# A linear-attention and MLP-mixer kernel on one core: Strassen products for the tail chunk, tail tokens twice in x, other engines for some evacuations, and an order written out job by job

## The chip, the cores and the metric

The kernel runs on one core of a Trainium2 chip. The metric is the device time of one execution in microseconds (us). Engines are named as in the profile: PE (TensorE), DVE (VectorE), ACT (ScalarE), POOL (GpSimd), SP (SyncE). Each has an instruction queue of its own that is worked off in order. A "bank" is one of PSUM's eight tiles of 128 x 512 fp32.

## The reference, cut to what matters

```python
def phi(x):                                   # q, k: batch 8, heads 8, tokens 576, head_dim 64; omega (128, 64)
    proj = einsum('bhsd,md->bhsm', x, omega)
    h = proj - sum(x*x, -1) / 2
    return exp(h - max(h, -1)) / sqrt(128)
q_p, k_p = phi(q * D**-0.25), phi(k * D**-0.25)
kv, z = einsum('bhsm,bhsd->bhmd', k_p, v), k_p.sum(2)
x = (einsum('bhsm,bhmd->bhsd', q_p, kv) / (einsum('bhsm,bhm->bhs', q_p, z) + 1e-6))   # -> (8, 576, 512)
h = relu(x.T @ w_tok1) @ w_tok2               # token mix, over the 576 tokens, 256 wide
u = x + h.T
out = u + relu(u @ w_ch1) @ w_ch2             # channel mix, 512 -> 1536 -> 512
```

## The kernel before, in words

The work is cut into eight batches. Of each batch's 576 tokens, 512 are its main part and 64 its tail. Main parts go through the channel mix as chunks 0 to 7; the tails of all eight batches together are a ninth chunk of 512 tokens, the tail chunk (chunk 8).

*Attention* (`attention`), per batch and pair of heads: kp (L729) and qp (L743) multiply by omega on 64 rows, one head on rows 0 to 63 and one on 64 to 127, side by side; L637 and L702 do so for the tails. ACT takes the exponentials (L605). DVE takes a maximum (km, L755) and its reciprocal, POOL scales v with it (vs, L762; for the tail vbd, L687), and PE makes kv from kp and vs (L775, L782), then the numerator and the denominator (num, L811 and L813). DVE divides and writes x (L820, L821). The fifth block of x holds the tail's 64 tokens; they stand on partitions 0 to 63 in even batches and on 64 to 127 in odd ones, beside rows made from a constant.

*Token mix* (`token_mix`): t1 is four matmuls with w1m and one with w1t per half of its output (L850, L851; in w1t the 64 rows of the other parity are zero), ACT's relu (L856), t2 (L868), then DVE's u = x + bank (L871). SP transposes u by DMA into uT (L876). Batch 0 has a form of its own (`token_mix_first`) that makes uT on PE. Every two batches, `token_tail` (L927) makes u of two tails.

*Channel mix* (`channel_mix`): c1 is 12 blocks of four matmuls of 512 columns on uT (L1031), each evacuated with a relu into r3 (L1051). For chunks 1 to 7, c2 is one level of Strassen's scheme (`channel_out_fast`): eight sums of halves of r3 on DVE (L961, tiles S and r3), then seven products of 12 matmuls of 256 columns (L994) in three banks, whose parts DVE reads and adds into the output tile o (L984). The sums of the weights (T1 to T4) are made once. Chunk 0 and the tail chunk use plain matmuls of 512 columns (L1072; the tail chunk's last quarter is split into 384 and 128), read by L1078 and L1081. SP stores o; the tail chunk's stores use SP and ACT.

*Loads.* Batches 0 and 1 come in through POOL's queue and are transposed on PE. For batches 2 to 7 POOL issues casts of q and k to fp16 in DRAM (L438, L443, L449), SP transposes them by DMA into qT and kT (L459), and POOL issues v (L416, and its tails, L430). Rings of three buffers hold qT, kT, v, x, u and uT.

*The order.* Each piece of work is a job with an engine, a cost, its dependencies, ring buffers that it takes and gives back, and a number from a list `TURN`. A planner (`Planner.run`) simulates the five engines with these costs and latencies and emits, of the jobs that could start first, the one with the lowest number; it fills PE's early waits with warm-up matmuls (L1124). Instructions then wait on semaphores where data or buffers demand it. POOL's loads are emitted in the order in which they are written. Three kinds of one-element POOL copies shape the loads in time: `touch_k` (L465) waits until kT of the batch has landed and stands ahead of that batch's load of v; `touch` (L471) waits until uT of batch b has landed, and the casts of batch b + 2 depend on it; `touch_u` (L477) waits for u of batch 1.

```python
load_transposed(b, b + key_of("lt", b), [touched.get(b - 2)])
load_v(b, b + key_of("lv", b), [touch_k(b, b + key_of("lv", b) - 0.05)] + ([touch_u(1, ...)] if b == NPE else []))
```

Of the kernel before, what the change touches and what calls it, by code (L numbers as in the profile page):

```python
# [21 lines left out]
TURN = [  # L22
    -15388, -7014, -13073, -46412, -7655, -14474, 12016, -15120, -18496, -8948, -22583, -7858, -7162, -43936, -2670,
    -3017, -3707, -7692, -13686, -20652, -22584, -5417, -6661, 23621, -1630, 152, -9786, 2937, -1379, -138, -4135,
    -255, 4012, -3019, 670, 2119, 30050, 19008, 6817, -16440, -9549, -63949, -1403, 26445, -14635, 15804, -8690,
    -63651, 24140, -58019, -2452, 24373, -36567, 21763, -1540, 3521, 18852, -60314, -19711, -30831, 6684, -19830,
    -11197, -21227, 25889, -24043, -11262, -14356, 3710, 6752, 14413, 23069, 5660, -15408, -27860, -2965, -7377,
    -9431, -12808, -52400, -38242, -37163, 3221, -15263, -20804, 22879, -13557, -55206, 13839, -49786, -6465, -202,
    4680, -47025, -14457, -46071, -53899, -9443, -9649, 8913, -19532, -37383, 814, -9792, -6427, -10267, -51100,
    15583, 27254, 1777, -46019, -50474, 376, 26739, 17561, -2105, -3193, 5465, -17463, 14213, -8969, 4853, -22951,  # L30
    19318, 1706, -24052, -49983, -13533, -6294, 24662, -12349, -49546, 5784, -3169, 5564, -50029, 26601, -30746,
    24843, -11451, -28569, -2751, 22527, 552, -6715, -14407, -15375, -15464, -19936, -52721, -17904, 3300, 12869,
    -15917, -13321, -9958, -1491, -4819, 646, -46682, -17992, -46784, -4826, 13594, -4048, 13343, 19470, 2741,
    -10090, 11772, 3497, -5567, -29390, 7254, 12676, 2776, -14376, 7802, 8337, 7031, -2161, -19859, -12732, -43413,
    -9916, -19216, -58973, 24369, -11565, 14103, -3033, -45480, -9352, 9592, 10185, -2540, 16827, 15484, -13557,
    -44120, -21483, -31242, -23901, 3400, -7003, -5296, -3805, -47459, -29837, -27877, -7451, -4247, 1753, -20557,
    2929, -1773, 21124, -1789, -25228, -1620, 18791, -664, -15420, -11225, -13389, -2744, 9408, 9845, 435, -135,
    22445, -3541, 13038, 5863, 20166, -10760, -19471, -21644, -601, -4056, -430, 14232, 4189, 10468, 10949, -3475,
    20422, -10178, 18794, -18465, -20798, 31084, -6838, 16566, 9681, -18602, 5577, 10752, -5297, -1849, 19149,
    -12929, -24198, -66020, -14908, -8184, -6166, -65205, 15276, -20150, 14963, -55181, -16990, -46958, -19935, 8099,  # L40
    -10665, 15556, 14406, 13591, 5438, -6274, 26511, 13520, 38954, 15603, -4947, 14565, 36526, 12763, 34929, 21853,
    37001, 15602, -6766, -6262, 14706, 15439, -13517, 15693, 21144, -1398, -6408, -6939, -8983, -13623, -8992, -9289,
    4719, -27010, -6574, -18136, 82, -2371, -17032, -9823, -27011, 8384, -6192, -16093, -17910, 7758, 14140, 108,
    -27948, -608, 8854, -3453, -10109, -11577, -13810, -12470, 3257, -14080, -8494, -10771, -11257, -16618, 3330,
    -17274, 3235, 1670, -16429, 7138, -2910, 2486, 3385, -13533, -59219, -9482, 8754, -17013, -8823, -6579, -11568,
    -9073, -5422, -2651, 5141, -1820, -13228, 11174, 2352, 10114, 10115, -14066, 1258, 4850, 33304, -25525, -22868,
    -25662, 1269, -8677, -14059, 7313, -16048, -12329, -4122, -16317, 2689, -25562, 22276, 4775, -18710, 10356, 496,
    -11758, 27399, -19583, 6689, -11186, -12765, -17338, -7597, -4698, -11639, -29139, -21982, 15114, -5787, -20076,
    -28319, -20689, -243, -14445, -11767, -19981, -10038, -5733, -16232, -14384, -3701, 6130, 4202, -3590, -23397,
    -3610, -22146, -2047, -7777, 3535, 11696, 3589, 14053, 2793, 349, 3537, 8491, 2220, -23014, 20063, -17210, 4249,  # L50
    11695, 709, 8460, 12020, 13969, -15424, 26804, -12046, 20202, -1874, 17391, 18744, -3467, -19446, 17390, -1859,
    16401, -22023, 9451, 4339, -22707, -17446, -26451, 2094, -15746, -4272, 14774, -19651, -7156, 112, -3587, -3434,
    -25433, 13873, 2630, 14048, -9769, 4425, -7075, -12087, -12522, -3917, 19581, -6390, -8901, -13427, -1181, 18678,
    -4045, 432, 13615, -5437, 13007, 1443, -10585, 9797, 2214, 7391, -2032, 12571, 1889, -3491, -6954, -29303,
    -23182, -29817, -24332, -2931, -7501, 14998, 8245, 10927, 2002, -11810, -21550, -14902, -7946, -26279, -1301,
    691, 11121, -3713, -6826, -4056, -2755, 26323, -554, 18902, -5970, -4993, -8453, -1366, 17640, 17804, 15115,
    19580, -5186, 6192, -134, 18765, 4162, 6381, 3651, 15911, 14780, -18160, -2045, 9672, -17660, 9621, -30386,
    -8188, -5144, -8187, -9411, 4616, 4852, 17834, 1462, -3139, 8840, -8896, 10423, -7338, 8960, 10376, -13163,
    17091, 13977, -8452, 16450, -30333, 9153, -8833, 13566, -28636, 10261, -5968, 9124, -2133, 30589, -41106, 8194,
    -1789, 1126, -6770, 5103, -6966, 8220, 1127, -17938, -9868, 11145, -13150, 10984, -2000, 29580, 27864, -15095,  # L60
    -4250, -10990, 13810, -46500, 13768, 21261, 18983, 2772, 2773, 3575, 16170, 30919, 2607, 14110, 16463, -2343,
    -18310, 8382, -7529, 16273, 30384, -516, 22171, -4626, -7305, 12970, 9221, 4737, -2165, -3253, 19048, 8805,
    10216, 19023, 13372, -12974, 11970, 19, 4449, -4866, 17204, -19334, -4013, 6176, -10560, -5347, 8886, -9214,
    -646, -5775, 6886, -8689, 1067, 6856, 3158, -2940, -8332, 5904, -7885, 13864, 6344, 8784, 6527, -8874, 3721,
    -206, -6079, -4129, 2648, -10216, 12686, 12078, -3004, -2224, 1638, -9213, -9825, -3812, 7751, -10988, -23199,
    -33491, 9689, -15345, -20536, -4352, -19859, 1333, -27862, -410, -18682, 15542, -7578, -16202, -5477, -6051,
    10330, 8738, 22953, -6008, 4920, -6176, -14218, 3475, 8079, -5905, -12788, 6217, 32716, -14997, 5159, 6270,
    25813, -10318, -10090, -5657, 7197, 7779, -13330, 7447, -8542, -9159, -3758, 22193, -6764, 27075, 6187, 8529,
    7206, 4308, 6524, -2156, 12129, -5827, -16280, -2630, 2881, 17984, 21000, 16285, 17051, 12562, -6502, -6544,
    -9527, 7971, 10323, 27175, -2021, 2054, 4848, -31261, -28426, -28130, -4079, 9328, -15259, 10054, -4167, -30516,  # L70
    -5759, -17236, 20912, -972, 4958, 21570, -3312, -18297, -2638, -50055, -1835, -47249, 413, -18400, -1670, -5520,
    -2170, -12900, 17150, 20837, -523, -31628, 6469, 112, -21361, 654, 18930, 13337, 6087, -6279, -2464, -8753,
    18192, 21341, 16066, -11343, -5800, -35522, 20880, 13337, -8965, 1896, -479, 1679, 5789, 288, -4811, 19118,
    25207, -1825, 11820, 16405, 20905, -43154, 11987, 27547, -4681, 10209, 8803, -2197, -8946, -3709, -17557, -8805,
    -10533, -16199, -27491, 16535, -8963, 26146, 1314, -18247, 9883, 6199, 1093, -19913, 4757, 16992, -476, 18685,
    -466, 9779, 4835, 4538, 16112, 22955, 25162, -26473, 1094, -15053, 8983, 23425, 18551, 15144, -2067, -14401,
    -25674, -3264, 19068, 21564, 19370, 21561, 19369, -369, 7251, 28795, 38558, 8305, -8220, 33607, 32424, -2369,
    -10808, -6295, -4563, -17410, -1230, 3456, 2605, 2422, 5647, 13207, 11405, 18208, 16281, -851, -32006, -9286,
    -3095, 9391, -1432, -1952, -5493, 20459, 11276, 9074, -1347, 12251, -21810, -7967, 8343, 6672, 9815, 569, -21526,
    15454, 8190, 9367, 7493, 16884, 728, 27655, -7207, -7903, 9589, 7508, 10012, 907, -13199, 6107, -5350, 16904,  # L80
    -4500, -12015, 7158, 26304, 6259, 24558, -3285, 10424, -716, -7436, -6436, -772, -35890, 3797, -17806, 10011,
    27243, 5135, 23103, -2409, -2140, -10265, 9455, 582, -7559, 6671, -13709, 2151, -15262, 8943, -20097, -5684,
    28560, -5089, -22380, 13833, -21820, -9450, 6234, 11702, 2636, -14448, -11523, 20648, 8829, -18231, -4520, 5423,
# [1073 lines left out]
```

## Time and profile before

| | |
|---|---|
| time, median of 3 runs | 282.66 us (282.34 to 283.93) |
| span of the profiled execution (first to last instruction) | 282.4 us; the page gives no other time of it |
| PE | busy 273.4 us (97%), granted clock 1.000 |
| DVE, ACT, POOL | busy 194.2, 158.6, 93.5 us |
| DMA | 39.63 MB, engines 0.8 to 1.0 busy for most of the first 200 us |
| first PE transposes start, last matmul starts | 4.67 us, 278.04 us |

The profile is one execution. "Busy" of PE counts modelled ends, and matmuls overlap by pipelining, so how long one holds the array is read from starts that follow each other. A chain line gives start, length, what, and a count. A group's or timeline's line gives line of the code, engine, operation, tile written <- tiles read, form, count, and in brackets the idle time before it with what ended it.

### The profile page before, as it was taken

Reading aid. Unit: us, or ns where it says so; the run is one execution under the profiler, and the core shown is the slowest. Engines: PE = TensorE matmul, PEld = TensorE weight load, DVE = VectorE, ACT = ScalarE, POOL = GpSimd, SP = SyncE. Lnnn points to the kernel's source line nnn. Section 1 sums busy time; section 2 is a strip of 40 time slices with the busy share of each in tenths; the row PEclk is TensorE's granted clock in tenths of the full one; section 3 lists DMA queues with packets and bytes.
Section 4 is the critical chain, followed back from the end, with each engine's and each line's share of the span. In section 5 each row is a group of like instructions: output and inputs, shape, how many; then the busy total and the mean of one; then the engine's idle time right before and its main releaser. Section 6 shows DMA issues by size and latency. Waiting matters only on the chain.

```text
span 282.4 us, 6126 instructions
## 1 busy us (share of the span) xinstructions
PE 273.4 (97%) x2437; PEld 166.1 (59%) x2437; DVE 194.2 (69%) x404; ACT 158.6 (56%) x329; POOL 93.5 (33%) x126
## 2 busy tenths in 40 slices
PE   7999999998999999999999999999999999999994
PEld 4577464443557656745567556655675477446761
DVE  3986959566798858694998576789796794034232
ACT  2987882098547663875576654875576511671200
POOL 8995950109312810256116501570151000000000
PEclk9999999999999999999999999999999999999999
DMA  8999999799963799989991997599963013300035
GB/s 190 199 202 191 202 217 160 176 190 148 229 91 77 155 190 151 124 217 148 157 151 61 205 209 110 105 194 228 149 91 152 0 22 74 149 2 0 0 151 149
DMA packets 83708, 39.63 MB, mean 140 GB/s; under 512 B 64160, under 2 KB 79904, under 8 KB 83488
## 3 DMA queue, kind: packets, MB, share of 16 engines
q0 software_dynamic: 34288, 17.45, 44.7%
q1 hardware_dynamic: 48608, 21.01, 33.3%
q10 hardware_dynamic: 784, 0.79, 0.9%
q8 instruction: 19, 0.31, 0.4%
q14 instruction: 9, 0.07, 0.1%
HBM read 35.88 MB, written 16.52 MB: 186 GB/s over the span
## 4 chain that ended last, share of the span: by engine, by line
PE 76%; DMA 9%; POOL 6%; DVE 6%; issue 2%; DVEq 0%; POOLq 0%
PE bank L1031 27%; PE bank L994 23%; PE bank L1072 5%; PE bank L850 4%; PE bank L868 4%; DMA uT<-u 3%; POOL vs L762 3%; DMA v<-in_v_dram 3%; DMA r<-in_k_dram 3%; PE bank L775 3%; PE bank L811 2%; DVE km L755 2%; PE bank L743 2%; PE bank L729 2%; PE bank L576 1%
## 5 line engine op out<-in xcount | busy, mean ns | idle before, releaser
L1051 ACT ACTIVATE r<-bank 128x512 f16<-128x512 f32 x106 | 63.0, 600 | 60.7 <-PE bank L1031 59.4
L1031 PE MATMUL bank<-uT,wc 128*128 128x512 f16 x376 | 88.6, 379 | 0.8 <-DMA uT<-u 0.8
L1031 PEld LDWEIGHTS <-wc 128*128 128x128 f16 x424 | 39.1, 98 | 41.0 <-DMA uT<-u 1.2
L605 ACT ACTIVATE qp<-bank 128x512 f16<-128x512 f32 x64 | 35.6, 624 | 19.1 <-PE bank L743 19.1
L755 DVE TENSOR_REDUCE km<-kp 128x8 f16<-128x1024 f16 x32 | 38.6, 1208 | 0.8 <-ACT kp L605 0.4
L605 ACT ACTIVATE kp<-bank 128x512 f16<-128x512 f32 x64 | 35.5, 627 | 6.3 <-PE bank L729 6.3
L762 POOL TENSOR_TENSOR vs<-v,vs 128x512 f16<-128x512 f16 x32 | 33.3, 1060 | 11.3 <-DVE vs L757 8.5
L994 PEld LDWEIGHTS <-r 128*128 128x128 f16 x336 | 32.2, 98 | 8.0 <-issue 1.3
L821 DVE TENSOR_TENSOR x<-bank,rc 128x320 f16<-128x320 f32 x62 | 30.5, 492 | 2.1
L984 DVE TENSOR_TENSOR o<-u,bank 128x512 f32<-128x512 f16 x28 | 19.0, 678 | 12.8 <-PE bank L994 12.8
L994 PEld LDWEIGHTS <-S 128*128 128x128 f16 x252 | 23.7, 98 | 6.3 <-issue 1.4
L820 DVE RECIPROCAL rc<-bank 128x5 f32<-128x5 f32 x62 | 11.6, 187 | 20.6 <-PE bank L813 19.6
L1072 PE MATMUL bank<-wc,r 128*128 128x512 f16 (+2 forms) x108 | 23.1, 356 | 0.0
L994 PE MATMUL bank<-wc,r 128*128 128x256 f16 x168 | 20.7, 273 | 0.0
L994 PE MATMUL bank<-T,r 128*128 128x256 f16 x168 | 20.7, 273 | 0.0
L994 PE MATMUL bank<-T,S 128*128 128x256 f16 x168 | 20.5, 273 | 0.0
L871 DVE TENSOR_TENSOR u<-x,bank 128x512 f16<-128x512 f16 x28 | 17.9, 682 | 1.2 <-PE bank L868 1.1
L687 POOL TENSOR_TENSOR vbd<-vt,vbd 128x512 f16<-128x512 f16 (+1 forms) x7 | 8.2, 1178 | 31.0 <-DVE vbd L678 8.0
L984 DVE TENSOR_TENSOR o<-o,bank 128x512 f32<-128x512 f32 x21 | 14.2, 676 | 6.0 <-PE bank L994 5.6
L465 POOL COPY junk<-kT 128x1 f16<-128x1 f16 x6 | 1.1, 189 | 49.3 <-DMA kT<-k 49.3
L961 DVE TENSOR_TENSOR S<-r 128x768 f16<-128x768 f16 x14 | 7.7, 552 | 13.7 <-ACT r L1051 13.6
L1072 PEld LDWEIGHTS <-r 128*128 128x128 f16 x108 | 9.9, 98 | 10.1 <-issue 0.7
(121 smaller groups left out, 391.1 us busy)
## 6 DMA issues: line engine op xcount, KB each, us to landing
out_dram<-o SPq DMA_DIRECT2D x14, 512.0 KB, 2.7
q<-in_q_dram POOLq DMA_DIRECT2D x6, 576.0 KB, 7.0
wc<-in_moe_w_ch_dram POOLq DMA_DIRECT2D x4, 768.0 KB, 12.0
k<-in_k_dram POOLq DMA_DIRECT2D x6, 512.0 KB, 8.1
v<-in_v_dram POOLq DMA_DIRECT2D x6, 512.0 KB, 6.5
r<-in_q_dram POOLq DMA_DIRECT2D x4, 256.0 KB, 7.2
v<-in_v_dram POOLq DMA_DIRECT2D x4, 256.0 KB, 7.2
out_dram<-o SPq DMA_DIRECT2D x4, 256.0 KB, 5.5
```

Source lines behind the costliest of these rows:

```text
L605: nc.scalar.activation(out=out, in_=in_, func=AF.Exp, bias=0.0, scale=1.0)
L755: nc.vector.reduce_max(out=mx, in_=kpv, axis=AX.X)
L762: nc.gpsimd.tensor_tensor(out=vs[:, :, 0:D], in0=t_v[place("v", b)][:, hh[0] : hh[0] + 2, :].rearrange("p h (j d) -> p (h j) d", d=D), in1 ...
L820: nc.vector.reciprocal(out=rc, in_=ps[:, :, :, D])
L821: nc.vector.tensor_tensor(out=t_x[place("x", b)][:, :, (2 * hp + hs[0]) * D : (2 * hp + hs[0] + n) * D].rearrange("p j (i d) -> p i j d", ...
L850: nc.tensor.matmul(ps, w1m[:, j, tb * P : (tb + 1) * P], x[:, j, :], start=(j == 0), stop=False)
L871: nc.vector.tensor_tensor(out=t_u[place("u", b)][:, j, :], in0=t_x[place("x", b)][:, j, :], in1=bank(n), op=ALU.add)
L984: nc.vector.tensor_tensor(out=o, in0=a, in1=ps, op=ALU.add)
L994: nc.tensor.matmul(ps[:, j * DH : (j + 1) * DH], a[:, cb, j * P : (j + 1) * P], w[:, cb, :], start=(b not in held and j == 0 and cb == 0), ...
L1031: nc.tensor.matmul(ps, wc1[:, db, cb * P : (cb + 1) * P], moving(db), start=(db == 0), stop=(db == ND - 1))
L1051: nc.scalar.activation(out=o, in_=bank(n), func=AF.Relu)
L1072: nc.tensor.matmul(ps[:, cols], r3[:, cb, j * P : (j + 1) * P], wc2[:, cb, cols], start=(cb == 0), stop=(cb == NCB - 1))
```

## The change

1. **Tail chunk by Strassen.** Chunk 8 goes through `channel_out_fast` too; the last of its seven products is split into two halves of six matmuls, with a read and a store each. u of the tails becomes one tile.
2. **Tail tokens twice in x.** qpt holds each tail token twice, so the fifth block of x has the tail on both halves of the partitions. w1t holds its 64 rows twice. For batches 1 to 7, t1's two matmuls with w1t become a pair on 64 rows each, ahead of the eight with w1m (jobs `t1_tail`). Batch 0 keeps a zero-padded copy (w1z).
3. **No copies that wait on DMA.** `touch_k`, `touch` and `touch_u` are gone. vbd of batches 0 and 1 moves into the tile T, and the constant rows of qpt are gone.
4. **Evacuations spread.** A table `MOVED` changes the engine of some 100 jobs: relus and copies between ACT and DVE, some vs from POOL to DVE, some Strassen sums from DVE to POOL, most stores of chunks 0 to 7 from SP to ACT's queue.
5. **New explicit order.** A list `ORDER` gives the jobs one by one over all engines (negative numbers are warm-up matmuls), and `SLOT` the ring buffers; no planner decides any more. POOL's loads may stand in any order.

The diff, cut to its core:

```diff
-    load_transposed(b, b + key_of("lt", b), [touched.get(b - 2)])
+    load_transposed(b, b + key_of("lt", b))
...
-    load_v(b, ..., [touch_k(b, ...)] + ([touch_u(1, ...)] if b == NPE else []))
+    load_v(b, b + key_of("lv", b))
...
+        for n in ORDER:
+            if n < 0:
+                self.warm(-1 - n)
+                continue
+            j = self.jobs[n]
...
+                    i = self.held[tag, name] = int(next(slots))
...
+    def engine(self, usual):
+        return MOVED.get(len(self.jobs), usual)
...
-    t_qpt = ring(COUNT["qpt"], [P, ST + SM + ST], FP16, "qpt")
+    t_qpt = ring(COUNT["qpt"], [P, H, 2, ST], FP16, "qpt")
...
-                exp(o[:, e], two(n_qt)[e][:, 0:256].rearrange("p (h r) -> p h r", h=H))
+                exp(o[:, e], two(n_qt)[e][:, 0:256].rearrange("p (h r) -> p h r", h=H).unsqueeze(2).broadcast_to((P, H, 2, RT)))
...
+        def t1_tail():
+            x = t_x[place("x", b)]
+            for tb in range(NT):
+                s = half[tb]
+                nc.tensor.matmul(bank(("h1", b, tb)), w1t[s, tb * P : (tb + 1) * P], x[s, NJ, :], start=True, stop=False)
...
-                    nc.tensor.matmul(ps, w1m[:, j, tb * P : (tb + 1) * P], x[:, j, :], start=(j == 0), stop=False)
-                nc.tensor.matmul(ps, w1t[:, b % 2, tb * P : (tb + 1) * P], x[:, NJ, :], start=False, stop=True)
+                    nc.tensor.matmul(ps, w1m[:, j, tb * P : (tb + 1) * P], x[:, j, :], start=False, stop=(j == NJ - 1))
...
-            on_act = c >= NPE or BY[("r0", "r1")[c]][cb] == "A"
+            e_relu = engine("ACT" if c >= NPE or BY[("r0", "r1")[c]][cb] == "A" else "DVE")
...
-                    (nc.gpsimd if on_pool else nc.vector).tensor_tensor(out=o[:, part], in0=a[:, part], in1=b[:, part], op=op)
+                    tt(e_sum, out=o[:, part], in0=a[:, part], in1=b[:, part], op=op)
...
-        fast = NPE - 1 <= c < B
+        fast = c >= NPE - 1
...
+            for j0, j1 in ((0, 1), (1, 2)) if tail and k == 6 else ((0, 2),):
```

More of the change, by code (lines that the diff above doesn't have):

```diff
@@ L228, in run @@
+        slots = iter(SLOT)
+        left, owner = {}, {}
+        for j in self.jobs:
+            for g in j.give:
+                left[g] = left.get(g, 0) + 1
+        for n in ORDER:
[3 more added lines that the diff above has]
+            j = self.jobs[n]
+            assert j.end is None and all(d.end for d in j.deps)
             for tag, name in j.take:
                 if (tag, name) not in self.held:
-                    i = self.find(tag)[0]
-                    self.places[tag][i] = math.inf
@@ L245, in run @@
+                    assert i < self.places[tag] and not left.get(owner.get((tag, i)))
+                    owner[tag, i] = (tag, name)
             j.fn()
+            j.end = True
             for g in j.give:
-                self.left[g] -= 1
-                self.freed[g] = max(self.freed.get(g, 0.0), j.end)
-                if self.left[g] == 0:
-                    self.places[g[0]][self.held[g]] = self.freed[g]
-        return max(at.values())
+                left[g] -= 1
+        assert all(j.end for j in self.jobs)
@@ L369, with copy, relu_to, tt @@
     src = {"q": q, "k": k}
+    def copy(eng, out, in_):
+        (nc.scalar.copy if eng == "ACT" else nc.vector.tensor_copy)(out=out, in_=in_)
+    def relu_to(eng, out, in_):
+        if eng == "ACT":
+            nc.scalar.activation(out=out, in_=in_, func=AF.Relu)
+        else:
+            nc.vector.tensor_relu(out=out, in_=in_)
+    def tt(eng, **kw):
+        (nc.gpsimd if eng == "POOL" else nc.vector).tensor_tensor(**kw)
     def bank(name):
@@ L661, in vbd @@
                 )
-            j_vbd0 = add("POOL", 2.15, HEAD["vbd"], vbd, deps=[j_mask, ld["vt", b]], take=[("vbd", b)], give=[("vt", b)])
+            e_vbd = engine("POOL")
+            j_vbd0 = add(e_vbd, 2.15, HEAD["vbd"], vbd, deps=[j_mask, *ld["vt", b]], take=[("vbd", b)] if dma_in else [], give=[("vt", b)])
         else:
@@ L989, in channel_out_fast @@
+        tail = c == B
+        outs = {}
         for k, (b, a_of, w, need) in enumerate(ops):
-            def go(k=k, b=b, a_of=a_of, w=w):
-                ps, a = bank((b, c)), a_of()
-                for j in range(2):
-                    for cb in range(NH):
-                        nc.tensor.matmul(ps[:, j * DH : (j + 1) * DH], a[:, cb, j * P : (j + 1) * P], w[:, cb, :],
-                                         start=(b not in held and j == 0 and cb == 0), stop=False, skip_group_check=True)
-                held[b] = True
@@ new lines, in channel_out_fast, with tail_rows, store @@
+        if tail:
+            def tail_rows(i, h, js, cols):
+                return out[4 * i : 4 * i + 4, SM:S, cols].rearrange("(j h) t d -> h t j d", h=2)[h][:, js, :]
+            ends = [(0, slice(0, 2), slice(0, DM), ["11", "12"], 0), (1, slice(0, 2), slice(DH, DM), ["22"], 0),
+                    (1, slice(0, 1), slice(0, DH), [("21", 0)], 0), (1, slice(1, 2), slice(0, DH), [("21", 1)], 1)]
+            for i, js, cols, need, two_queues in ends:
+                for h in range(2):
+                    eng = engine("ACT" if two_queues and h else "SP")
+                    def store(i=i, js=js, cols=cols, h=h, eng=eng):
+                        (nc.scalar if eng == "ACT" else nc.sync).dma_start(out=tail_rows(i, h, js, cols), in_=t_o[place("o", (c, i))][half[h], js, cols])
+                    dma(eng, key + 0.9, 0.3, store, deps=[outs[x] for x in need], give=[("o", (c, i))], cost=0.41)
+            return
@@ L1020, in channel_mix, with store @@
+        for i, need in ((0, ["11", "12"]), (1, [("21", 0), "22"])):
+            eng = engine("SP")
+            def store(i=i, eng=eng):
+                (nc.scalar if eng == "ACT" else nc.sync).dma_start(out=out[c, 0:SM, :].rearrange("(p j) d -> p j d", j=NJ)[:, 2 * i : 2 * i + 2, :], in_=t_o[place("o", (c, i))])
+            dma(eng, key + 0.9 + 0.1 * i, 1.3, store, deps=[outs[x] for x in need], give=[("o", (c, i))], cost=0.4)
     def channel_mix(c, key, jt):
@@ new lines, in channel_mix, with out_copy, store @@
+            k2 = key + 0.5 + 0.5 * (3 * j + 3) / 12
+            e_out = engine("DVE")
+            def out_copy(j=j, n=n, e_out=e_out):
+                copy(e_out, t_o[place("o", (c, j // 2))][:, j % 2], bank(n))
+            jo = add(e_out, 0.69, k2, out_copy, deps=[prev], take=[("o", (c, j // 2))], give=[("bank", n)])
+            eng = engine("SP")
+            def store(j=j, eng=eng):
+                (nc.scalar if eng == "ACT" else nc.sync).dma_start(out=out[c, j * P : (j + 1) * P, :], in_=t_o[place("o", (c, j // 2))][:, j % 2])
@@ L1094 @@
+            dma(eng, k2, 0.65, store, deps=[jo], give=[("o", (c, j // 2))], cost=0.4)
     for i in range(4):
```

430 lines of the change are left out of this document (148 added, 282 removed), and 134 rows, old and new, of tables (ORDER, TURN).

## The prediction

> **What bounds the kernel now.** I read the page first, parts 1 and 2.
>
> ```profile
> span 282.4 us, 6126 instructions
> PE 273.4 (97%) x2437; PEld 166.1 (59%) x2437; DVE 194.2 (69%) x404; ACT 158.6 (56%) x329; POOL 93.5 (33%) x126
> PEclk9999999999999999999999999999999999999999
> ```
>
> TensorE is busy 97% of the span at the full granted clock. So a gain has to come from fewer cycles in the matmul stream, or from its few gaps. Busy time hides how long a matmul holds the array, because ends are modelled (379 ns for 512 columns, L1031). The chain of waits, in order of time, shows it (start, length, what, count):
>
> ```profile
> 82.34 0.54 PE bank L743 x4
> ...
> 85.50 2.73 PE bank L994 x24
> ...
> 93.99 0.86 PE bank L1031 x4
> ...
> 271.21 7.17 PE bank L1072 x44
> ```
>
> Four matmuls of 512 columns take 0.86 us, so 0.216 each; 24 of 256 columns take 2.73, so 0.109 to 0.114 each. The 44 at the end are 24 of 512, 8 of 384 and 12 of 128; with 0.216, 0.163 and 0.056 they make 7.16, which is what stands there. L743 works on 64 rows in pairs: two pairs in 0.54, so 0.216 for a pair, and about 0.1 left for the change of form. The starts in the trace say the same: 0.205 from a 256-column matmul of L994 to the first of L743, against 0.109 within L994. A change between 128-row and 64-row (or 64-column) form costs 0.096.
>
> Then the gaps: the timeline of POOL around one, and PE's line behind it.
>
> ```profile
> 62.43 0.18 POOL L471 COPY junk<-uT 128x1 f16<-128x1 f16 x1 [7.86 <-DMA uT<-u]
> 63.26 0.53 POOL L438 DMA_DIRECT2D q<-in_q_dram  x1 [0.65 <-issue]
> 63.82 0.88 POOL L449 DMA_DIRECT2D k<-in_k_dram  x1
> 65.09 0.83 POOL L449 DMA_DIRECT2D k<-in_k_dram  x1 [0.39 <-issue]
> 65.91 0.55 POOL L443 DMA_DIRECT2D k<-in_k_dram  x1
> 66.48 1.07 POOL L687 TENSOR_TENSOR vbd<-vt,vbd 128x512 f16<-128x512 f16 x1
> 67.48 0.69 POOL L430 DMA_DIRECT2D vt<-in_v_dram  x1
> 68.19 4.09 POOL L762 TENSOR_TENSOR vs<-v,vs 128x512 f16<-128x512 f16 x4
> ```
> ```profile
> 62.35 2.76 PE L1031 MATMUL bank<-uT,wc 128*128 128x512 f16 x12 [0.22 <-DMA uT<-u]
> ...
> 69.30 0.40 PE L775 MATMUL bank<-vs,kp 128*128 128x65 f16 x8 [1.17 <-POOL vs L762]
> ```
>
> POOL sits in a one-element copy until uT has landed, then issues the next batch's loads for 5 us, and only then scales v for the kv matmuls; PE waits at 69.30. The same order stands at 122.95 to 127.49, with PE waiting until 128.61. I measured PE's gaps as start to start beyond the matmul's own cost and a change of form. After 35 us they are 0.55 (at 35.00), 0.64 (61.75 and 62.35, the second for uT), 1.33 and 0.25 (69.30, 71.32), 0.27 (77.42), 0.62 (122.87, for uT) and 0.76 (128.61): 4.4 us. After 130 there is none over 0.15.
>
> **The change, part by part.** Sums are against the profiled span of 282.4; the median, 282.66, stands 0.26 above it.
>
> *Tail chunk by Strassen.* Away: 36 matmuls of 512, 12 of 384, 12 of 128: 7.78 + 1.96 + 0.67 = 10.40 us. New: 84 of 256 at 0.109 = 9.16. Gain 1.2. Eight sums (0.47 each from start to start, L961) and eight reads of 0.28 to 0.69 replace DVE reads of 2.9; DVE is idle most of that stage, but the order at the end is serial. After the last c1 matmul come a relu (0.1 wait and 0.6), the four sums of the second half (about 2.0), and the first bank's read (0.7), since DVE's queue holds it behind the sums: 3.4 us. PE has M0 and one product of chunk 7 to do meanwhile, 2 x 1.31 = 2.6. So PE waits about 0.8 to 0.9: I take +0.9 (bounds 0 and 2). Behind the last matmul the read shrinks from 384 columns (0.55) to 256 (about 0.37, between the rows for 128 and 384), but the last store's issue stands behind another's on both queues (0.5): 0.
>
> *Tail tokens twice in x.* Batches 1 to 7 drop 14 matmuls of 512 at full rows (L851, 3.02 us) for 7 pairs of 64 rows at 0.22 = 1.54: gain 1.5. ACT's 16 exponentials for qpt grow from 256 to 512 columns, 0.30 to 0.48 from start to start, 2.9 us on an engine at 56%: nothing; without that cover 0.2 on each qpt.
>
> *New order on PE.* In the order of the program I count 88 changes of form before and 77 after, the pairs of the tail included (six of the seven follow another 64-row pair). 11 x 0.096 = gain 1.1. Six of 22 warm-up matmuls go, five of them behind the first transposes: 1.1 us if nothing else waits there. That stage waits for loads, so I take 0 and keep 1.1 in the range.
>
> *No copies that wait.* Twelve POOL copies of 0.19 go, and with them waits of 49.3 (L465), 11.0 (L471) and 13.2 (L477), which cost only where work was queued behind. In the changed order one issue of 0.5 us stands between vbd and the first vs of batches 2 and 4, and the others lie 9 us of matmul work or more ahead. So I take out 1.33 + 0.25 + 0.76: gain 2.3 (bounds 0 and 2.3). These copies also kept loads from running beside uT; that returns below as a rival.
>
> *uT's cover.* From t2's last matmul (L868) to the first c1 of the same batch PE has this much work, batches 1 to 7: before 9.5, 8.9, 10.5, 11.1, 11.1, 10.6, 10.0; after 6.9, 8.1, 8.7, 8.3, 9.2, 9.3, 11.3. uT needs about 1.7 from the last t2 to its issue, then 4.3 to 9.5 to land (median 6.0): it was 8.6 and 9.5 where a load of v started beside it (53.6 and 112.5), 4.3 alone. In the new order, by the matmul work between them, the nearest loads ahead of uT are v's by 12.7 and 7.6 (batches 1 and 2), a cast of k by 4.1 (batch 3) and one of q by 5.2 (batch 4); the next casts follow 2 us behind, and in batch 4 a load of v by 2.4. So I take 6.0: 7.7 is needed, and only batch 1 falls short, by 0.8, against 1.26 of gaps now: gain 0.4.
>
> *Evacuations.* 42 relus of 512 columns go to DVE against 2 (0.605 from start to start), with five more kvsb and 12 vs on DVE; 12 Strassen sums, 7 copies go off it. DVE's start-to-start sum rises from 185 to 212 us. Between the t1 of batches 5 and 6 it is 26.6 against PE's 28.9, before 22.2 against 29.0. No stretch of the order gives DVE more than 1.8 us beyond PE's work (before 2.2), and eight banks hold more than that; ACT stays at 143. I take +0.5 for reads that now queue behind relus (bounds 0 and 4). vs on DVE has no row: between 0.29 and 0.60 by the rows for 256 and 512 columns. A sum on POOL has none either: 1.5, between 1.06 for 512 and 1.94 for 1024. Twelve stores of chunks 0 to 7 go to ACT's queue, 0.6 each by the row of L1091; relus and exponentials stand behind them, so a store that waits for DVE holds those, and PE wants their banks. ACT has half its time free: 0. The first loads change places (both halves of wc1 behind batch 1's k and q); c1 of chunk 0 moves behind batch 1's first attention, so I take 0 (bounds -1 and +2).
>
> Sum: 282.4 - 1.2 - 1.5 - 1.1 - 2.3 - 0.4 + 0.9 + 0.5 = 277.3, and 0.26 on top: 277.6.
>
> **The rivals.** *uT late (slower).* Without the copies the casts and v's loads run on, and uT lands 9 us after its issue as it did at 53.69 and 113.29. Then 10.7 is needed, and covers of 6.9, 8.1, 8.7, 8.3 and 9.2 fall short by 3.8, 2.6, 2.0, 2.4 and 1.5: 12.3 in five batches instead of 0.8. That gives 277.6 + 11.5 = 289; with half of the batches hit, 284. It decides from a landing of about 7 us on. For it: the two slow landings above, DMA at 0.84 to 0.99 of its time between 80 and 200 us, covers shortened everywhere but in batch 7. Against it: only a load that started within 1 us of uT made it so slow (6.05 with v's load 3.5 ahead), and the order places none so near. Chance 0.18.
>
> *DVE in the way.* With 85 to 92% of PE's time in the middle, DVE's queue delays x and relus by a few tenths at each of some ten places, and PE by 3 us in all: 280.5. [...] Chance 0.18, of which the hold 0.08.
>
> *All gaps close.* The warm-ups' 1.1, uT's and the other gaps go as well and the end doesn't wait: 277.6 - 1.1 - 0.8 - 0.8 - 0.9 - 0.5 = 273.5. Chance 0.10.
>
> *Only the cycles count.* The new order makes other gaps as large as those it closes, and 282.66 - 3.8 = 278.9 is left: within the forecast's range.
>
> **How the numbers follow.** Forecast 277.6 with its own range 275 to 280.3: chance 0.54. About 0.5% (1.4 us) is what a measurement can tell from no change, so same is 281.2 to 284.1. Faster: 0.54 + 0.10 + half of DVE's 0.18 = 0.73. Same: 0.07 from DVE's other half and 0.03 from a mild case of late uT, 0.10. Slower: 0.15 from late uT and 0.02 from DVE, 0.17. The range goes from 273.2 to 284.5, which leaves out about 0.05 below and 0.14 above.
>
> **What would show it.** Right: PE's matmul stream shorter by 3.8 us, kv matmuls of batches 2 and 4 with no wait for POOL, c1 of batches 2 to 6 with no wait for uT, one wait near 0.9 before the tail's third product. Wrong: gaps before L939 with uT as releaser (the first rival), POOL sums or DVE sums longer than 1.5 and 0.56 where they meet, or PE waiting for DVE's x and relus (the second). A later first c1 of chunk 0 or c2's first matmul past 43 us would mean that the loads were reordered for the worse.

## The result, and the profile after

The changed kernel takes 290.73 us (median of four runs, 288.75 to 292.07), the kernel before beside it 283.30 (282.34 to 284.01): a ratio of 1.0262, 95% interval 1.0205 to 1.0318. It is slower. The profiled execution took 288.75, its span 287.0; what follows is read from it, and the 2 us by which the median lies above it are not explained by it; the three other executions show a granted clock of 0.985 to 0.990, this one 0.996. Ratios here and below leave out runs in a second, slower state of the chip: one kernel below spreads from 285.8 to 300.5, and its counted runs only to 289.3.

Page of the changed kernel, parts 1, 2 and 4; the same lines of before stand in the prediction.

```profile
span 287.0 us, 6120 instructions
...
PE 268.8 (94%) x2455; PEld 167.1 (58%) x2455; DVE 231.6 (81%) x453; ACT 138.7 (48%) x287; POOL 101.4 (35%) x115
...
PEclk9999999999999999999999999999999999999998
...
PE 65%; DVE 15%; DMA 9%; ACT 3%; issue 3%; POOL 3%; DVEq 0%; SPq 0%; POOLq 0%
```

TensorE has less to do and waits more. With the prediction's measure (start to start beyond a matmul's own cost and a change of form) the stream itself went from 269.7 to 263.8 us, the gaps from 7.1 to 15.2, and the stretch from the last matmul's start to the end of the span from 4.3 to 6.7: -5.9 + 8.1 + 2.4 (rounded) make the 4.6 that the span grew. What ended the gaps is in the table of waits (total, times, longest):

```profile
PE bank L889 <- DVE o L877: 6.1, 6, 2.1
...
PE bank L631 <- DMA kT<-k: 1.1, 1, 1.1
...
PE bank L939 <- DMA uT<-u: 0.5, 1, 0.5
PE bank L676 <- POOL vs L296: 0.3, 1, 0.3
```

The waits for POOL's scaling of v (2.3 before, at 69.30, 71.32 and 128.61) are gone, as forecast. New are the waits for L877, the read of a Strassen bank: as gaps 1.97 at 83.19, 1.09 at 173.20, 0.99 at 231.22 and 2.22 at 272.50, each ahead of a chunk's third product. This is DVE's line, and then POOL's, ahead of the first:

```profile
74.27 2.72 DVE L296 TENSOR_TENSOR r<-r 128x768 f16<-128x768 f16 x1
76.92 0.68 DVE L293 TENSOR_SCALAR r<-bank 128x512 f16<-128x512 f32 x1
77.70 2.44 DVE L296 TENSOR_TENSOR S<-r 128x768 f16<-128x768 f16 x1
...
80.94 0.55 DVE L296 TENSOR_TENSOR r<-r 128x768 f16<-128x768 f16 x1
```
```profile
73.98 0.92 POOL L338 DMA_DIRECT2D v<-in_v_dram  x1
74.92 1.65 POOL L296 TENSOR_TENSOR S<-S,r 128x768 f16<-128x768 f16 x1
...
77.15 0.90 POOL L338 DMA_DIRECT2D v<-in_v_dram  x1
78.07 1.65 POOL L296 TENSOR_TENSOR S<-r,S 128x768 f16<-128x768 f16 x1
```

A DVE sum that takes 0.55 alone takes 2.72 and 2.44 here. Each ends 0.42 after the POOL sum beside it has ended (76.57 and 76.99; 79.72 and 80.14). In the whole span eight DVE sums take 0.79 to 2.72, all eight lie beside POOL sums, and each ends 0.4 after one. DVE's share of the chain is 15%, against 6% before.

The end of the span, after and then before (SPq and ACTq are the store issues of the two queues, the last DVE line is the last read):

```profile
276.94 0.69 DVE L877 TENSOR_TENSOR o<-ut,bank 128x512 f32<-128x512 f16 x1 [2.24 <-DMA out_dram<-o]
...
279.30 2.63 SPq L919 DMA_DIRECT2D out_dram<-o  x4
279.31 3.35 ACTq L919 DMA_DIRECT2D out_dram<-o  x4
...
280.56 0.42 DVE L877 TENSOR_TENSOR o<-ut,bank 128x256 f32<-128x256 f16 x1
```
```profile
274.36 5.21 SPq L1091 DMA_DIRECT2D out_dram<-o  x7
274.37 5.12 ACTq L1091 DMA_DIRECT2D out_dram<-o  x3
...
278.40 0.55 DVE L1081 TENSOR_TENSOR o<-ut,bank 128x384 f32<-128x384 f16 x1 [0.61 <-PE bank L1072]
```

Both kernels store a megabyte of tail rows. Before, it leaves from 274.36 on while the matmuls run, and the span ends 3.4 us after the last read. After, nothing leaves before 279.30, and the span ends 6.0 after the last read.

### The profile page after: what moved, and what is told of

It reads as the page before. It is cut to its first block, busy times and chain, and to the rows that moved or that the text cites. A ratio compares the mean times of both kernels' runs of the same rounds, so it can differ in the third digit from the quotient of the medians.

```text
span 287.0 us, 6120 instructions
## 1 busy us (share of the span) xinstructions
PE 268.8 (94%) x2455; PEld 167.1 (58%) x2455; DVE 231.6 (81%) x453; ACT 138.7 (48%) x287; POOL 101.4 (35%) x115
## 4 chain that ended last, share of the span: by engine, by line
PE 65%; DVE 15%; DMA 9%; ACT 3%; issue 3%; POOL 3%; DVEq 0%; SPq 0%; POOLq 0%
PE bank L939 27%; PE bank L889 18%; DMA kT<-k 4%; DVE S L296 4%; PE bank L973 4%; PE bank L676 3%; DVE u L768 3%; DMA uT<-u 2%; DMA v<-in_v_dram 2%; DVE o L877 2%; DVE r L296 2%; PE bank L709 2%; PE bank L765 2%; PE bank L643 2%; PE bank L631 2%
## 5 line engine op out<-in xcount | busy, mean ns | idle before, releaser
L291 ACT ACTIVATE r<-bank 128x512 f16<-128x512 f32 (+1 forms) x81 | 46.2, 604 | 78.7 <-PE bank L939 62.6
L889 PEld LDWEIGHTS <-r 128*128 128x128 f16 x384 | 37.0, 98 | 8.6 <-issue 2.1
L293 DVE TENSOR_SCALAR r<-bank 128x512 f16<-128x512 f32 (+1 forms) x45 | 29.2, 664 | 8.7 <-PE bank L939 6.1
L889 PEld LDWEIGHTS <-S 128*128 128x128 f16 x288 | 27.9, 98 | 12.2 <-issue 7.3
L296 POOL TENSOR_TENSOR S<-r,S 128x768 f16<-128x768 f16 x7 | 12.6, 1801 | 59.5 <-DVE S L296 53.3
L296 POOL TENSOR_TENSOR vs<-v,vs 128x512 f16<-128x512 f16 x20 | 21.7, 1086 | 30.5 <-DVE vs L657 26.0
L877 DVE TENSOR_TENSOR o<-u,bank 128x512 f32<-128x512 f16 x28 | 19.0, 678 | 9.0 <-PE bank L889 8.9
L889 PE MATMUL bank<-T,r 128*128 128x256 f16 x192 | 23.8, 273 | 0.4 <-DVE o L877 0.4
L296 POOL TENSOR_TENSOR vbd<-vt,vbd 128x512 f16<-128x512 f16 x6 | 6.3, 1054 | 35.8 <-DVE vbd L579 35.8
L709 PEld LDWEIGHTS <-qp 128*128 128x128 f16 x256 | 13.7, 98 | 7.4 <-issue 0.2
L877 DVE TENSOR_TENSOR o<-o,bank 128x512 f32<-128x512 f32 x24 | 16.0, 672 | 1.3 <-PE bank L889 1.1
L296 POOL TENSOR_TENSOR S<-r 128x768 f16<-128x768 f16 x3 | 4.9, 1634 | 29.9 <-ACT r L291 23.3
```

Of the source, the lines that this page charges most:

```text
L291: nc.scalar.activation(out=out, in_=in_, func=AF.Relu)
L293: nc.vector.tensor_relu(out=out, in_=in_)
L296: (nc.gpsimd if eng == "POOL" else nc.vector).tensor_tensor(**kw)
L709: nc.tensor.matmul(ps[:, k, j * 65 : (j + 1) * 65], st, s[:, i, 0 : D + 1], start=True, stop=True)
L877: nc.vector.tensor_tensor(out=o, in0=a, in1=ps, op=ALU.add)
L889: nc.tensor.matmul(ps[:, j * DH : (j + 1) * DH], a[:, cb, j * P : (j + 1) * P], w[:, cb, :], start=(b not in held and j == 0 and cb == 0), ...
```

## The experiments

Theory: sums on POOL hold DVE's sums, and the end lost time to late stores. Rival: DVE simply has too much queued. Ratios are to the kernel before on the same chip, with their intervals; spans and waits are those of one profiled execution of each kernel.

**Sums back on DVE.** The twelve entries `303: "POOL"` and so on of MOVED taken out. (The ten sums that the expectation names are eight, as counted above.)

> The changed kernel with its twelve Strassen sums back on DVE, all else and the order of every queue as changed. If POOL's sums hold DVE's (ten DVE sums in the changed kernel's trace end 0.02 to 0.4 us after the POOL sum beside them and take up to 2.7 instead of 0.55), all DVE sums take 0.55 again, TensorE's waits for the read of L877 ahead of the third product go in the middle (1.97 at 83, 1.09 at 173, 0.99 at 231), and the one at the end falls from 2.2 to about 0.9: span 287.0 - 4.05 - 1.35 = 281.6, time about 284 (283 to 286, the changed kernel's own runs spread by 3). If instead DVE simply has too much queued work (relus and vs moved to it), twelve more sums of 0.47 make it worse: the waits for L877 stay or grow, time 290 to 294.

Ratio 1.0726 (1.0658 to 1.0794), span 300.4: worse than either theory had it. Waits of this kernel (its lines are numbered one higher):

```profile
PE bank L632 <- DMA kT<-k: 7.0, 2, 6.5
PE bank L644 <- DMA qT<-q: 6.8, 1, 6.8
PE bank L890 <- DVE o L878: 2.2, 4, 1.3
```

The waits for the read fell from 6.1 to 2.2. Ahead of the third products the gap at 173 became 0.58, the one at 231 went, and the one at the end fell from 2.22 to 1.49. With twelve more sums for DVE none grew, so the rival is out at these three places. At 83 a new wait just ahead hides the place; in two kernels below that have the sums on DVE and wait less than 0.9 there (the copy ahead of v's loads, and v for batch 4 later), no gap over 0.05 stands at that product. But two new waits came, for transposed loads. Queues of SP and POOL, first in the changed kernel, then with the sums on DVE:

```profile
64.87 4.97 SPq L381 DMA_TRANSPOSE qT<-q  x1
...
70.65 3.98 SPq L381 DMA_TRANSPOSE kT<-k  x1
...
71.72 1.63 POOL L296 TENSOR_TENSOR S<-r 128x768 f16<-128x768 f16 x1 [8.63 <-ACT r L291]
...
73.98 0.92 POOL L338 DMA_DIRECT2D v<-in_v_dram  x1
```
```profile
65.18 8.35 SPq L382 DMA_TRANSPOSE qT<-q  x1
...
74.33 9.13 SPq L382 DMA_TRANSPOSE kT<-k  x1
...
64.10 0.93 POOL L339 DMA_DIRECT2D v<-in_v_dram  x1
65.02 0.63 POOL L353 DMA_DIRECT2D vt<-in_v_dram  x1
65.64 0.91 POOL L339 DMA_DIRECT2D v<-in_v_dram  x1
```

In the changed kernel POOL's queue stops at a sum until ACT's relu is there (8.63 us), and the load of v behind it starts at 73.98. With no sum in the queue, two loads of v start at 64.10 and 65.64, beside qT and kT, and the transposed loads keep SP 1.7 and 2.3 times as long. So the sums on POOL have a second effect, a good one: they hold loads back.

**A sum that nobody reads.** This tells the two effects apart: DVE does all sums, and at each of the twelve places POOL does one beside DVE's whose result nobody reads, written to places of uTt and, in the tail chunk, of x. (Late ones fall on places then in use, so the tail tokens' output is changed.)

```
 o, a, b = what()
+if at in BESIDE:
+    x = r3(0, 0) if k0(at) else a
+    nc.gpsimd.tensor_tensor(out=unread[c == B], in0=x[:, part], in1=b[:, part], op=op)
 tt(e_sum, out=o[:, part], in0=a[:, part], in1=b[:, part], op=op)
```

> All Strassen sums on DVE, and a sum that nobody reads on POOL at each of the twelve places where the changed kernel had one: same size, its operands the sum's own or finished as early, output to an unused tile. Nothing on DVE or TensorE depends on it. If the mere presence of a two-input sum on POOL holds DVE's two-input sums, DVE sums of 1.2 to 2.4 us stand beside the POOL sums again and the waits for L877 come back: 3 to 6 us over the kernel with the sums on DVE alone, 287 to 290. If the changed kernel lost time because a POOL sum takes 1.6 instead of 0.47 within a chain of four that depend on each other, nothing is slower than with the sums on DVE alone: within 0.7 of it.

Ratio 1.0629 (1.0557 to 1.0700), span 297.5. DVE's line and POOL's:

```profile
76.04 1.42 DVE L301 TENSOR_TENSOR r<-r 128x768 f16<-128x768 f16 x1
...
78.64 1.99 DVE L301 TENSOR_TENSOR S<-r 128x768 f16<-128x768 f16 x1
```
```profile
75.39 1.65 POOL L862 TENSOR_TENSOR uTt<-S,r 128x768 f16<-128x768 f16 x1
...
78.55 1.65 POOL L862 TENSOR_TENSOR uTt<-r,S 128x768 f16<-128x768 f16 x1
```

At all twelve places a DVE sum took 0.93 to 2.00 instead of 0.55, though nothing depends on POOL's. TensorE's waits for DVE's reads, x and relus came to 13.8 us (7.3 + 2.8 + 2.3 + 1.4), and its waits for qT and kT are gone. So the hold is shown by itself, and the holding back of loads too. By the ratios the time is 2.7 us below that with the sums on DVE, by intervals that overlap, and not 3 to 6 above it as expected, since the second effect was not in the expectation.

**The same sums in the kernel before.** There the eleven of chunks 1 to 6 are issued on POOL: `on_pool=(c, g, k) in ON_POOL` in the sum's function, order as it was.

> The kernel before with one edit: the eleven sums of chunks 1 to 6 that the changed kernel gives to POOL go to POOL here too, order and all else as before. If POOL sums hold DVE's, the DVE sums beside them take up to 2.4 us, and TensorE, which had no wait for DVE in the chunks before, waits 0.5 to 2 us in about half of these places: 285 to 290. If only the changed kernel's fuller DVE queue (81% against 69%) makes them harmful, the time is within 1 of the kernel before.

Ratio 1.0100 (1.0069 to 1.0131), as the hold has it, at its lower edge. Its waits:

```profile
PE bank L998 <- DVE o L988: 1.6, 2, 1.2
PE bank L871 <- DVE u L874: 1.4, 1, 1.4
```

Neither stands in the table of before. Five DVE sums beside POOL's took 1.34 to 1.99.

**The kernel before without its copies.** The prediction's step alone: the twelve `tensor_copy` to junk left out, nothing else.

> The kernel before with one edit: the twelve POOL copies that wait for a DMA are gone, with their order of all else as it was. The prediction's step took 2.3 us off for this (the waits for POOL's scaling of v at 69.30, 71.32 and 128.61): 280 to 281. If the copies' use was to keep the loads of v and the next casts away from the transposed loads, waits for qT, kT or uT of 2 to 7 us come in their place: 285 to 293.

Ratio 1.0684 (1.0624 to 1.0743): 19 us slower, where the prediction's step had 2.3 faster. A wait of 0.2 for POOL's vs is left of 2.3, but:

```profile
PE bank L743 <- DMA qT<-q: 12.0, 3, 11.4
PE bank L702 <- DMA qT<-q: 3.8, 2, 2.3
```

The qT of batch 2 was issued at 44.32 beside a load of v (38.93) and the next cast of q (41.79), both of which the copies had held until 53.60 and 63.26; it landed 22.6 us later, against 6.0 before.

**A copy in each sum's place, and a new end.** Sums on DVE; on POOL a copy of one column of each of the twelve results, so that its queue stops there but sums nothing. Then the same with the tail's end rewritten; that end also on the kernel with the sums alone.

```
 tt(e_sum, out=o[:, part], in0=a[:, part], in1=b[:, part], op=op)
+if at in TOUCHED:
+    nc.gpsimd.tensor_copy(out=junk, in_=o[:, part][:, 0, 0:1])
```
```
-("X", lambda: s_of(2), T2, last),
+("X", lambda: s_of(2), T2, sums[2]),
...
-in_=t_o[place("o", (c, i))][half[h], js, cols]
+in_=t_o8[place("o", (c, i))][half[h], js, cols]
...
+ends = [(0, slice(0, 2), slice(0, DH), ["11"], 1), (1, slice(0, 2), slice(DH, DM), ["22"], 1), (0, slice(0, 2), slice(DH, DM), ["12"], 1),
```

> The twelve Strassen sums on DVE, and on POOL, at each of the twelve places, a copy of one column of the sum's result instead. So POOL's queue still stops there until the sum is done, and the loads behind it are issued no earlier than that; but POOL has no two-input sum of 128x768 any more. If the sums on POOL cost time by holding DVE's, and the kernel with the sums on DVE lost its 14 us only because the loads of v, no longer held back by POOL's queue, ran beside the transposed loads of q and k (8.35 and 9.13 us instead of 4.97 and 3.98), both are gone: no wait for qT or kT of 6 us, no wait for L877 over 0.5 in the middle, 0.9 at the end: 281.6 as a span, 283 to 286 as a time. If the loads need more holding back than a copy gives (a sum on POOL held them 1.1 us longer), one or both waits of 6 us come back: 289 to 300.

> The kernel with the sums on DVE, and the tail's end rewritten as well: the tail's outputs in tiles of their own, the read of the first product between the sums, the third product waits for its own sum only, the last product of Z ahead of the last two halves of X, and five pairs of stores, each issued behind its read. If the end of the changed kernel lost 2.4 us because its megabyte of stores was issued in the last 3.4 us (the span ends 6.0 after the last read, against 3.4 before), the span ends about 3.5 after the last read, and the gap ahead of the third product is 0.2 to 0.4: 2.5 to 3 us less than with the sums alone, 281 to 282. If the stores at the end were limited by something else (the clock, the landing of small stores), the time is within 0.7 of the kernel with the sums alone.

> The same with the tail's end rewritten as in the kernel with the sums and the end, which took 3.5 us off the kernel with the sums alone: 2.2 between the last matmul and the end of the span, 1.1 ahead of the third product. The same again here: 280 to 282.5, 1 to 3 us under the kernel before. If the granted clock or the landing of the stores takes it back, within 1 of the kernel with the copies alone.

With the copies the ratio fell from 1.0726 to 1.0206 (1.0138 to 1.0274), and no DVE sum takes more than 0.56; this agrees with both effects. Against the changed kernel's 1.0262 the intervals overlap: the waits for DVE's reads fell, but one of 3.1 for kT came, so a net gain from the sums' leaving POOL is not shown. With the new end as well it is 1.0103 (1.0070 to 1.0136), with an interval below the changed kernel's: the best kernel of this study, still slower than before. On the kernel with the sums alone the ratio went from 1.0726 to 1.0661 (1.0573 to 1.0749), far from the 281 to 282 us expected, as the waits for qT and kT stayed (6.4 and 6.2). The spans, 300.4 and 295.9, show what the end does: 3.2 of their difference lie there, 1.0 in gaps between the last products and 2.2 behind the last matmul. The end of the kernel with the copies and the new end:

```profile
270.39 0.68 DVE L884 TENSOR_TENSOR x<-ut,bank 128x512 f32<-128x512 f16 x1
...
276.93 4.43 SPq L926 DMA_DIRECT2D out_dram<-x  x5
276.93 4.70 ACTq L926 DMA_DIRECT2D out_dram<-x  x5
...
279.77 0.75 DVE L884 TENSOR_TENSOR x<-ut,bank 128x256 f32<-128x256 f16 x2 [0.62 <-PE bank L896]
```

The read (now into a tile of x) stands between the sums, the gap ahead of the third product is gone, the stores start 2.8 us ahead of the last two reads, and the span of 284.2 ends 3.7 after them. For the tail's second product (c2), take its matmuls, the gaps among them, and the stretch behind the last: before 10.4 + 0 + 4.3 = 14.7, in the changed kernel 9.2 + 2.2 + 6.7 = 18.1, here 9.2 + 0.5 + 4.7 = 14.4. So Strassen for the tail lost 3.4 us as changed, and gained 0.3 when well ordered. One wait of 3.1 for kT was left, at 81.35.

**Chasing the waits that are left.** Four kernels, the first made from the last one: a copy ahead of each load of v on POOL that waits for the last q or k transposed; from there the 44 relus back on ACT; the first with the load of v for batch 4 behind kT; that with DVE's queue reordered.

```
 def main():
+    if landing:
+        nc.gpsimd.tensor_copy(out=junk, in_=landing[-1][:, H * RA - 1 : H * RA])
     nc.gpsimd.dma_start(out=t_v[place("v", b)][:, h0:h1, :], ...
```

> The kernel with the copies and the new end, and ahead of each load of v on POOL's queue one more copy, of the last column of the q or k that was transposed last, so that the load of v starts only when that has landed: the kind of copy that the change took out. In the kernel with the copies, kT of batch 3 took 10.1 us to land beside a load of v issued 3.4 later, and TensorE waited 3.2 for it at 81.35. If the removed copies' use was to keep v's loads away from the transposed ones, this wait goes and nothing comes for it: span 284.2 - 3.2 - 0.7 (clock regained) = 280.3, time 281.5 to 282.5. If v then lands too late for POOL's scaling of it, TensorE waits there instead, 1 to 3 us: 283 to 286.

> The kernel with both kinds of copies and the new end, and the 44 relus that the change moved from ACT to DVE are back on ACT. If DVE's fuller queue costs the waits for DVE that are left (0.41 at 109, 0.69 at 114, 0.58, 0.26 and 0.30 at 174 to 181, 0.28 at 202), they go: 2 to 2.5 us under the kernel with both kinds of copies, 279.5 to 280.5. If ACT, which then has the relus, the exponentials and the stores' issues in one queue in an order made for less, is late with banks, waits for ACT come instead: the same or up to 5 more.

> The kernel with both kinds of copies and the new end, and the load of v for batch 4 moved on POOL's queue from ahead of batch 3's uT to behind batch 4's kT. In the kernel with both kinds of copies, two loads of v stood at 79.13 and 80.91, uT, issued at 83.80 beside them, took 12.2 us to land instead of 4.3, and TensorE waited 5.9 for it. With one load of v there uT should take 4.5 to 6: the wait goes to 0 to 0.5, span 282.3 to 282.8, time 283.5 to 284.5. If uT is slowed by the casts behind it rather than by v, the wait stays above 3: 286 to 288.

> The same, and DVE's queue reordered at the places where TensorE still waits for it: three reads of chunk 4 ahead of work that is not yet wanted, one sum of chunk 2 behind an x, three relus of token mixing back on ACT. These waits were 0.58, 0.26 and 0.29 at 178 to 185, 0.41 at 113, 0.70 at 118 and 0.28 at 206, 2.5 in all; with them gone the time is 1.5 to 2.5 less than with the later load of v alone: 281 to 283, 0 to 2 under the kernel before. If these waits only pass to the next one behind them, it is within 0.7 of the kernel with the later load alone.

Ratios 1.0197 (1.0147 to 1.0246), 1.0182 (1.0157 to 1.0207), 1.0152 (1.0106 to 1.0197) and 1.0187 (1.0129 to 1.0244): none reached the gain that it aimed at, and their intervals overlap. Each wait aimed at went or shrank, and another came. The wait for kT fell from 3.1 to 0.7, but uT of batch 2 (the expectation of the next kernel calls it batch 3's), now beside two loads of v, took 12.2 us and TensorE waited 5.7 for it; the relus on ACT took the waits for DVE's relus away (0.8) and changed the time by less than can be told; with the load of v moved that uT was in time, but the next one, beside casts, cost 3.4; with DVE's queue reordered the waits for DVE fell to 0.9, but kT and uT took 6.5.

**All loads behind waiting copies, twice.** The copies in the place of every load of batches 3 to 7, as before had them, and the casts of batches 5 to 7 moved behind uT; then those of batches 6 and 7, and two loads of v, moved behind the vbd and vs that TensorE wants first.

> The kernel with the later load of v and the reordered DVE queue, and the waiting copies in the place of every load of batches 3 to 7, as the kernel before had them: the casts of q and k of a batch stand behind a copy of uT of two batches before, each load of v behind a copy of that batch's kT (qT for batch 5); the casts of batches 5 to 7 and two loads of v are moved behind these. The kernel it is made from had waits of 3.0 (kT), 3.7 (uT), 0.3 (uT) left, and its runs spread from 285.8 to 300.5. If it is loads beside the transposed ones that make both, the waits go and the spread falls to that of the kernel before (2 us): span 279 to 281, time 280 to 282.5. If the copies, with POOL's vs and vbd queued behind them, make TensorE wait for POOL as in the kernel before (2.3 there), 282 to 284. If the transposed loads are slow for another reason, waits for them over 2 us stay: over 285.

> The kernel with all the waiting copies, and the casts of batches 6 and 7, their kT and the loads of v for batches 6 and 7 each moved behind the vbd and vs that TensorE wants first. In the kernel with all the copies every uT landed in 4.3 to 6.0 us and no wait for uT was left, but vbd and vs stood on POOL's queue behind the copies and TensorE waited 25.0 us for them (14.3 and 8.4 in two places). If that was the placing alone, 22 to 25 of the 32 us that it was slower go: 315.8 - 24 = 292, and 283 to 286 where the waits for kT (2.9) and qT (2.7), that came with it, go too. If POOL cannot hold loads back and scale v in time in this order at all, TensorE waits for POOL over 8 us in other places: over 296.

Ratios 1.1149 (1.1099 to 1.1198) and 1.0562 (1.0505 to 1.0618). Waits of the first, and of the second:

```profile
PE bank L699 <- POOL vbd L307: 15.7, 2, 14.3
PE bank L692 <- POOL vs L307: 9.3, 3, 8.4
```
```profile
PE bank L659 <- DMA qT<-q: 3.7, 1, 3.7
PE bank L553 <- DMA kT<-k: 3.2, 1, 3.2
PE bank L647 <- DMA kT<-k: 1.9, 1, 1.9
PE bank L620 <- DMA qT<-q: 1.7, 1, 1.7
PE bank L692 <- POOL vs L307: 1.4, 3, 0.5
```

Every uT landed in 4.3 to 6.0, so loads beside it were what made it slow. But with the copies in front, POOL's own work was late; with that work first, POOL's waits fell from 25.0 to 1.4, and qT and kT were late by 10.5 in four places: their casts now wait for uT, and this order asks for them sooner than casts and transposes take. Whether an order exists that keeps the saved cycles and has time for the loads stays open.

## Why the prediction was wrong, by its steps

*The cycles were right.* 3.8 was forecast for the tail's products, the pairs and the forms; the stream is 5.9 shorter, of which the six warm-ups (0.21 each) are 1.3. The other 0.8 is the start's half rate: the first transposes start 0.213 apart until 7.04 before, eleven of them, and only two do so now, ahead of 4.75; from there on they start 0.109 apart, so nine make 0.9. This is no gain of the change: in the two kernels above that are made from the one before, the half rate ends at 6.1 and 7.3.

*The step that failed first: the evacuations (+0.5).* It sized a sum on POOL by its length alone (1.5; it took 1.63 to 2.04) and gave the hold, a POOL sum that keeps a DVE sum beside it waiting, 0.08 as a part of a rival. That was an estimate of mine that no trace of before shows: there no DVE sum lies beside POOL's scaling of v, and every one takes 0.55 to 0.56; in the changed kernel the eight held ones took 0.79 to 2.72. The three gaps in the middle are 4.05, of which 0.58 at 173 stays when DVE does the sums; with 0.7 of the one at the end (2.2 with the sum on POOL, 1.5 with it on DVE) the price of the sums on POOL, their length and the hold together, is 4.2. The rival that had DVE in the way counted 3 in all, with a chance far too low. In the kernel before, eleven of these sums on POOL cost 2.8 by the ratio; the sum that nobody reads shows that the hold alone brings such waits. The row was missing in the trace of before because POOL never ran a sum there, and that was no reason to think it unlikely. A vs on DVE took 0.64 to 0.69 by itself, above the bounds taken (0.29 to 0.60).

*The second: the end (-1.2 + 0.9 + 0).* The gap came out as 2.2: the 0.7 of hold, and 0.6 that the serial sum had too short. And the last store was booked at nothing because one issue was thought to stand behind another. The point was missed that Strassen's outputs, in this order, are complete only near the end, so the whole megabyte is issued then: +2.4. Forecast 0.3 shorter in all, the tail came out 3.4 longer.

*The third: the removed copies (-2.3).* The gaps went, but the reason was wrong. The copies' waits were counted as idle time of POOL that costs what is queued behind; their use, to start loads late, was left to the rival of late uT. Without them the kernel before is 19 us slower. In the changed kernel the sums on POOL do part of their work; what got past is a kT that took 11.4 us at 99.57 and cost 1.24 at 111.03.

*The first loads (0, bounds -1 and +2).* Gaps ahead of 30 us are 6.1 against 2.5; with the six warm-ups' 1.3 taken off, 2.3 more. The longest single one is 0.84 at 10.65, for a load of q; no run tells which change of the order did it.

*uT and the reads* came as forecast: 0.68 of gap (0.8), though in batch 4, where uT took 6.72, and not in batch 1, where it took 4.32: that size agrees by luck. DVE's reads cost 0.55 at 176 and 180 (0.5 was forecast), and the 0.58 at 173 belongs with them.

The sum with what was measured: 277.3 + 4.05 + 1.3 + 2.4 + 1.24 + 2.3 = 288.6; less 0.8 of shorter stream and 0.8 of gaps that the sum had kept (0.55 at 35.00, 0.27 at 77.42), 287.0. The rival that ended slower, late uT at 289, had the time but not the cause: uT cost 0.68. DVE in the way, at 280.5, had the largest cause, in the hold, but not the time: the rest of the end, the first loads and kT came on top with 6.5. The rival that only the cycles count assumed new gaps as large as the old; they were twice as large.

## What to carry to other kernels

Before you take out a wait that seems to cost only its own engine, ask what it delays behind it: a queue that stops may be what keeps loads apart. Before you move a sum to a spare engine, measure one beside the busy engine's work; and when a product completes its outputs late, count the stores that then come together.

## What the runs showed of the hardware that I had not expected

*POOL and DVE.* In the changed kernel a DVE sum with two SBUF inputs that met a POOL sum and ended behind it did so by 0.4 us, and a POOL sum that started behind a DVE sum took up to 2.04 instead of 1.63. DVE's reads of a bank (0.68 at 110.16), its relus (0.68 at 109.56) and its reductions of one input (km, 1.21 at 170.55) took their usual time beside POOL sums. Six of the eight held sums started behind POOL's. The two longest, by their recorded starts, began 0.65 and 0.37 ahead of POOL's sum, while POOL issued a load of v (73.98 and 77.15), and still ended after it. A DVE sum beside the issue of a cast alone took 0.56 (107.67). What decides there stays open.

*Transposed loads.* In the kernel before, uT took 4.3 us by itself (85.82), and 8.6 and 9.5 beside a load of v (53.69, 113.29); with the copy ahead of v's loads it took 12.2 beside two of them. qT took 4.7 at the least in the changed kernel (51.43), and 22.6 at the most, in the kernel before without its copies.

*The clock after a wait.* With the sums on DVE, TensorE waited 6.9 us for qT at 82.25. By windows of that kernel (length, busy times of PE, PEld, DVE, ACT and POOL, then granted clock, DMA share, GB/s):

```profile
78.00:82.00 4.00, 0.00 (x0) 0.00 (x0) 2.25 (x5) 0.00 (x0) 0.00 (x0) 0.58 1.35 212
82.00:85.00 3.00, 2.75 (x10) 0.87 (x11) 0.00 (x0) 1.77 (x3) 0.00 (x0) 0.50 1.24 215
85.00:88.00 3.00, 2.51 (x20) 1.16 (x19) 0.00 (x0) 1.64 (x4) 0.00 (x0) 0.92 0.23 88
88.00:92.00 4.00, 4.00 (x33) 2.76 (x33) 2.84 (x5) 1.90 (x4) 0.00 (x0) 1.00 0.00 0
```

The granted clock is 0.50 for the first 3 us of work after the wait, so by an estimate from these 3 us it costs some 1.5 us more than its own time. Behind the wait of 6.7 for kT at 124.04 it is 0.50 until 129.8, some 2.9 more; behind the wait of 3.1 at 81.35 in the kernel with the copies and the new end, until 84.6 (its page shows 0.7 in the slice from 78.2 to 85.3).
